# Outgoing sums in another pool's buffers, tied fetches, a gated conversion and one mask tile in a scan with two experts

## The chip, the cores and the metric

One core of one Trainium2 chip. The metric is the device time of one launch in microseconds, the median of three runs; a profiled execution of its own gives the trace.

## The reference

An attention with a running state, then two feed-forward experts one after the other on all 3072 tokens. Weights and inputs of the experts come as float64, the attention's as float32; all results are float32.

```
state = zeros(B, H, D, D)                       # B=4, H=8, D=40, S=768 steps
for t in range(S):
    y[:, :, t] = einsum('bhd,bhde->bhe', r[t], state)
    Sa = einsum('bhde,bhe->bhd', state, a[t])
    state = state * w[t][..., None, :] - einsum('bhd,bhe->bhde', Sa, b[t])
    state = state + einsum('bhd,bhe->bhde', v[t], k[t])
x = y as (3072, 320)
h = x @ w_in                                    # expert one, 320 x 2048
x = (max(h, 0) + alpha * min(h, 0)) @ w_out     # 2048 x 320
g = x @ w_gate                                  # expert two, 320 x 1536
out = (g * sigmoid(g) * (x @ w_val)) @ w_out2   # 1536 x 320
```

## The kernel before, in words

**Stages.** The 768 steps are cut into six blocks of 128 (`NM`), each in chunks of 64 (`L`), so that a block's scan is a row of matmuls with short steps of ScalarE and VectorE between them. Expert one of a block (512 tokens, `mlp1(j)`) can begin when the block's attention is there, and runs beside the scan of the following blocks to fill TensorE. Blocks 4 and 5 are left when the scan ends. Expert two runs over all six blocks at the end.

**Precision.** Each float32 factor is split into a high part and the rest (`split`: a copy on ScalarE, a subtraction on VectorE or GpSimd), and a product is a sum of three, so that one tile of 128 hidden units costs eight up matmuls (`up_mm`) and eight down matmuls (`down_mm`). An up product goes to the PSUM tile `u`, of which there is one in the scan and three afterwards; `prelu` makes `g` and its parts `gh`, `gl` from it; the down products are summed over the 16 tiles `f` of a block in `d0`, `d1`, `d2`.

**Weights.** A float64 weight is loaded as two words of 32 bits and made into a float32 by `narrow`: two operations on ScalarE, two on VectorE, in tiles `wy` (one buffer) and `wz` (two). `conv` then splits it. Expert one's converted weights go to a DRAM tile `wd` and are fetched as `wt` for each block (four buffers, `WB`); the tiles `f10` to `f15` are fetched in block 4 into tiles that stay for block 5 (`resident`, pool `hold`). Of expert two, four of twelve tiles are converted during the scan (`conv2`, 12 conversions, fetched back later) and 24 conversions (`direct`) follow after the scan straight into their resident tiles `w0`, `w1`, `w2`, some of them within expert two's first block.

**Sums of expert one.** At a block's end the three sums are copied from PSUM to a tile `x1o` and written to DRAM (`x1d`), two by ScalarE and the third, which adds two halves, by ScalarE and VectorE. `x1o` has the tag `xa`, the staging tile through which the next block's `x` is loaded (`fill_x`, three buffers). `g` has a pool `gp1` of two buffers, but is itself cut to one.

**Order.** The program is written as generators that `drive` interleaves by shares; a list scheduler then places each instruction by priority and by when its inputs and buffers come free, and every engine runs its own instructions in the order so found. All transfers named here are issued by SyncE, except the attention's stores `xd`, issued by ScalarE. A change of a pool's buffers moves instructions on all engines. `issue_after` is a tie in this scheduler: an instruction inside it is placed behind the named one where both are issued by one engine.

Of the kernel before, what the change touches and what calls it, by code (L numbers as in the profile page):

```python
# [39 lines left out]
ZB = 2  # L40
# [7 lines left out]
YB = 1  # L48
# [15 lines left out]
L = 64  # L64
HALF = 32
LOOK = 2
KEEP = 4

@with_exitstack
def kernel(  # L70
# [94 lines left out]
    def narrow(pool, raw):  # L165
# [8 lines left out]
        nc.vector.scalar_tensor_tensor(z, z, 3, y, ALU.logical_shift_left, ALU.bitwise_or)  # L174
        return f

    def split(raw, h, l, eng):
        nc.scalar.copy(out=h, in_=raw)  # L178
        eng.tensor_tensor(out=l, in0=raw, in1=h.bitcast(F32), op=ALU.subtract)  # L179

    def conv(stage, idx, src, f, kind, into=None):
        sw = words(src)
        if kind == "up":
            raw = stage.tile([128, 3, 128, 2], U32, tag="raw", name="raw", bufs=RB)
            sw = sw[:, f * 128:f * 128 + 128]
            nc.sync.dma_start(out=raw[:, 0:2], in_=sw[0:256].rearrange("(j p) n two -> p j n two", p=128))
            for p in (lo, hi):
                nc.sync.dma_start(out=raw[p, 2], in_=sw[256:DM])
        else:
            raw = stage.tile([128, DM, 2], U32, tag="raw", name="raw", bufs=RB)  # L190
            nc.sync.dma_start(out=raw, in_=sw[f * 128:f * 128 + 128])
        w32 = narrow(stage, raw)
        t = stage.tile([128, 768], F32R, tag="wc", name="wc", bufs=WCB) if into is None else into
        if kind == "up":
            t3 = t.rearrange("p (a b) -> p a b", a=6)
            split(w32, t3[:, 0:3], t3[:, 3:6], nc.gpsimd)
        elif kind == "down":
            split(w32[:, 0:256], t[:, 0:256], t[:, 256:512], nc.gpsimd)
            split(w32[:, 256:DM], t[:, 512:512 + RT], t[:, 512 + RT:2 * DM], nc.gpsimd)
        else:  # L200
            split(w32, t[:, 0:DM], t[:, DM:2 * DM], nc.gpsimd)
        if into is None:
            n = 768 if kind == "up" else 2 * DM
            nc.sync.dma_start(out=wd[idx, :, 0:n], in_=t[:, 0:n].bitcast(F32))

    fetched = []
    e1p = {}
    XAB = [XAB1]

    resident = {}  # L210

    def fetch(pool, idx, up, j):
        if idx in resident and j == NM - 1:
            return resident[idx]
        n = 768 if up else 2 * DM
        if j == NM - 1 or j == NM - 2 and idx >= 2 * HOLD:
            tag = f"w{idx // 2 % 2}" if up else "w2"
            t = e1p["hold"].tile([128, n], F32R, tag=tag, name="wt")
            resident[idx] = t.rearrange("p (a b) -> p a b", a=6) if up else t
        else:  # L220
            t = pool.tile([128, 768], F32R, tag="w", name="wt")
        fetched.append(nc.sync.dma_start(out=t[:, 0:n].bitcast(F32), in_=wd[idx, :, 0:n]))
        return t.rearrange("p (a b) -> p a b", a=6) if up else t

    def up_mm(ps, t, xs):
        xh, xl, xst = xs
        ops = []
        for j in range(2):
            ops += [(t[:, j], xh[:, j]), (t[:, j], xl[:, j]), (t[:, 3 + j], xh[:, j])]
        ops += [(t[:, 2], xst), (t[:, 5], xst)]  # L230
        for i, (lt, rh) in enumerate(ops):
            nc.tensor.matmul(ps, lt, rh, start=(i == 0), stop=(i == len(ops) - 1))  # L232

    def down_mm(ps, q, t, gh, gl, first, last):
        if q < 2:
# [31 lines left out]
        return xs  # L267

    def prelu(gpool, ps, f, n):
        g = gpool.tile([128, n], F32, tag="g", name="g", bufs=1)  # L270
        nc.scalar.activation(out=g, in_=ps, func=ACTF.Relu, scale=-1.0)  # L271
        nc.vector.scalar_tensor_tensor(g, g, neg[:, f:f + 1], ps, ALU.mult, ALU.add)  # L272
        gh = gpool.tile([128, n], F32R, tag="gh", name="gh")
        gl = gpool.tile([128, n], F32R, tag="gl", name="gl")
        split(g, gh, gl, nc.gpsimd if f % 16 < PGL else nc.vector)
        return gh, gl
# [18 lines left out]
    def mlp1(j, early=0):  # L295
# [5 lines left out]
        plan += [(f, 0, BLK) for f in fs if f >= early]  # L301
        dps = [psd.tile([128, BLK], F32, tag=f"d{q}", name=f"d{q}") for q in range(3)]
        pend = []

        def down(f, c0, c1, gh, gl):
            t = fetch(wp1, 2 * f + 1, False, j)
            for q in range(3):
                down_mm(dps[q][:, c0:c1], q, t, gh, gl, f == fs[0] and c0 == 0, f == fs[-1])

        seen = set()  # L310
        for f, c0, c1 in plan:
            if not seen & {(c0, c1), (0, half) if early and c0 == 0 else (c0, c1)}:
                with lifted():
                    b0, b1 = c0 // TB, c1 // TB
                    fill_x(xp1, xs, xd[j][:, b0:b1].rearrange("f b t -> f (b t)"), c0, c1)
                seen.add((c0, c1))
                yield
            t = fetch(wp1, 2 * f, True, j)
            ps = e1p["psu"].tile([128, c1 - c0], F32, tag="u", name="u")
            up_mm(ps, t, tuple(x[..., c0:c1] for x in xs))  # L320
            yield
            if len(pend) == DEP:
                down(*pend.pop(0))
            pend.append((f, c0, c1, *prelu(gp1, ps, f, c1 - c0)))
            yield
        for e in pend:
            down(*e)
        for q in range(3):
            tc.cur_priority -= XPRI
            o = xp1.tile([128, BLK], F32, tag="xa", name="x1o", bufs=XAB[0])  # L330
            if q < 2:
                nc.scalar.copy(out=o, in_=dps[q])
                nc.sync.dma_start(out=x1d[j][q * 128:q * 128 + 128], in_=o)
            else:
                nc.scalar.copy(out=o[lo], in_=dps[2][hi])
                nc.vector.tensor_tensor(out=o[lo], in0=dps[2][lo], in1=o[lo], op=ALU.add)
# [20 lines left out]
    WN = NSEG * (L + 1)  # L357
    wseg = rawp.tile([128, WN + 1], F32, name="wseg")
    nc.vector.memset(wseg[:, 0:WN + 1:L + 1], 0.0)
    reset = rawp.tile([128, NSEG // 2, L + 1], F32, name="reset")  # L360
    nc.gpsimd.memset(reset, 0.0)
    nc.gpsimd.memset(reset[:, :, 0:1], 1.0)
    first = rawp.tile([128, NSEG, L + 1], F32, name="first")
    nc.gpsimd.memset(first, 0.0)
    rests = [rawp.tile([128, NSEG, L + 1], F32, name=f"rest{j}") for j in range(2)]
    mask = pers.tile([128, L], F32, name="mask")

# [124 lines left out]
    def prep_a(i):  # L492
# [8 lines left out]
        for g in range(2):  # L501
# [395 lines left out]
    def direct():  # L897
        for f in range(KEEP, K2):
            for j, (held, src, kind) in enumerate(KINDS):
                t = wpool.tile([128, 768 if kind == "up" else 2 * DM], F32R, tag=f"w{j}", name=f"w{j}")  # L900
                conv(tail, 2 * K1 + 3 * f + j, src, f, kind, t)
                held[f] = t.rearrange("p (a b) -> p a b", a=6) if kind == "up" else t
                yield

# [123 lines left out]
```

## Time and profile before

| | us |
|---|---|
| median of 3 runs | 1274.12 (1267.84 to 1275.93) |
| profiled execution | 1273.08 |
| its span | 1271.0 |
| TensorE busy in it | 1110.3 |
| mean granted clock of TensorE | 0.929 of full |

The span is the time from the first to the last instruction that the profile shows; the profiled execution's own time has about 2 us outside it. In the rows PE is TensorE, DVE VectorE, ACT ScalarE, POOL GpSimd and SP SyncE. A row of a timeline is a run of equal instructions, and its bracket says how long the engine had been idle before and what released it.

### The profile page before, as it was taken

The page shows a single profiled execution, that of the slowest core. Times are in us where ns is not written, and L with a number is a line of the kernel's source. Part 1 is how long each engine was busy: PE and PEld are TensorE (multiplying, and loading weights), DVE is VectorE, ACT ScalarE, POOL GpSimd, SP SyncE. Part 2 cuts the span into 40 slices and gives each one's busy share as a digit, 9 for nine tenths or more (in the row PEclk, how much of TensorE's full clock was granted, in tenths as well). Part 3 has the DMA queues.
Part 4 walks back from the last instruction along what each step waited for, and adds up shares of the span by engine and source line. Part 5 has one row for each costly group of instructions (what it writes and reads, how often), then busy time and mean ns, then how long its engine had stood idle before and what let it go on. Part 6 is the DMA issues. An engine that isn't in the chain of part 4 may idle for free. (4 is left out here: it accounts for less than half of the span.)

```text
span 1271.0 us, 24355 instructions
## 1 busy us (share of the span) xinstructions
PE 1110.3 (87%) x9056; PEld 940.2 (74%) x9056; DVE 728.2 (57%) x1552; ACT 619.3 (49%) x1531; POOL 236.1 (19%) x405
## 2 busy tenths in 40 slices
PE   4146687999999989999899678998999999999998
PEld 4045676887777877787688555877888888888887
DVE  7798887688498579759554344457532323232222
ACT  4659468647745754863844334447432323232222
POOL 8336433311221221331321000003100000000000
PEclk9668677999999998999899889999999999999999
DMA  4535778555444554635765698245210101000000
GB/s 142 169 94 171 255 258 264 166 179 165 135 146 147 150 149 130 205 101 153 234 202 150 223 345 286 72 127 154 67 46 1 46 1 38 1 21 1 13 9 21
DMA packets 94885, 166.36 MB, mean 131 GB/s; under 512 B 13232, under 2 KB 43184, under 8 KB 94768
## 3 DMA queue, kind: packets, MB, share of 16 engines
q1 hardware_dynamic: 86608, 160.88, 40.1%
q10 hardware_dynamic: 8160, 3.93, 1.1%
q8 instruction: 72, 1.18, 0.4%
q14 instruction: 45, 0.37, 0.1%
HBM read 136.98 MB, written 27.79 MB: 130 GB/s over the span
## 5 line engine op out<-in xcount | busy, mean ns | idle before, releaser
L178 ACT CAST gh<-g 128x512 fp32r<-128x512 f32 (+1 forms) x176 | 105.6, 600 | 179.7 <-DVE g L964 120.5
L232 PE MATMUL u<-xh,wt 128*128 128x512 f32 (+1 forms) x416 | 153.1, 412 | 26.4 <-ACT xh L178 15.0
L179 DVE TENSOR_TENSOR gl<-g,gh 128x512 fp32r<-128x512 f32 (+1 forms) x176 | 118.6, 674 | 96.2 <-ACT gh L178 94.5
L964 DVE TENSOR_TENSOR g<-pv,sg 128x512 f32<-128x512 f32 x72 | 49.8, 692 | 215.6 <-PE pv L232 213.4
L272 DVE SCALAR_TENSOR_TENSOR g<-g,neg,u 128x512 f32<-128x512 f32 (+1 forms) x104 | 73.1, 703 | 96.4 <-ACT g L271 96.2
L232 PEld LDWEIGHTS u<-xh,wt 128*128 128x128 f32 x416 | 82.5, 202 | 50.2 <-ACT xh L178 15.7
L962 ACT ACTIVATE sg<-pg 128x512 f32<-128x512 f32 x72 | 43.0, 598 | 133.4 <-PE pg L232 133.4
L271 ACT ACTIVATE g<-u 128x512 f32<-128x512 f32 (+1 forms) x104 | 58.7, 565 | 98.3 <-PE u L232 70.5
L232 PE MATMUL pg<-xh,w 128*128 128x512 f32 x288 | 102.0, 394 | 3.6 <-ACT sg L962 3.6
L232 PE MATMUL pv<-xh,w 128*128 128x512 f32 x288 | 100.5, 389 | 0.0
L948 PE MATMUL o<-w,gh 128*128 128x320 f32 x288 | 87.3, 309 | 0.6 <-ACT gh L178 0.6
L949 PE MATMUL o<-w,gh 128*128 128x320 f32 x288 | 87.7, 309 | 0.0
L232 PE MATMUL u<-xl,wt 128*128 128x512 f32 (+1 forms) x208 | 82.8, 398 | 0.2 <-DVE xl L179 0.2
L238 PE MATMUL d<-gl,wt 128*128 128x512 f32 (+1 forms) x208 | 82.2, 397 | 0.0
L609 DVE TENSOR_TENSOR la<-la,tmp 128x96 f32<-128x96 f32 (+43 forms) x306 | 80.2, 290 | 2.0
L696 POOL COPY gs<-raw_v 64x160 f32<-64x160 f32 x96 | 45.1, 470 | 190.5 <-PE yp L753 94.9
L239 PE MATMUL d<-gh,wt 128*128 128x512 f32 (+1 forms) x208 | 80.2, 387 | 0.0
L601 DVE TENSOR_TENSOR tmp<-la 128x96 f32<-128x96 f32 (+43 forms) x306 | 78.9, 284 | 1.8
L540 PE MATMUL mnp<-AN,kbt 128*128 128x128 f32 x384 | 60.0, 309 | 22.6 <-DVE kbt L528 13.5
L950 PE MATMUL o<-w,gl 128*128 128x320 f32 x288 | 76.1, 309 | 0.0
L237 PE MATMUL d<-gh,wt 128*128 128x512 f32 (+1 forms) x208 | 70.9, 395 | 5.7 <-DMA wt<-wd 4.3
L554 POOL TENSOR_SCALAR_AFFINE_SELECT AN<-AN 64x256 f32<-64x256 f32 x96 | 51.5, 537 | 123.8 <-ACT AN L553 105.1
(116 smaller groups left out, 2575.8 us busy)
## 6 DMA issues: line engine op xcount, KB each, us to landing
wt<-wd SPq DMA_DIRECT2D x98, 384.0 KB
wt<-wd SPq DMA_DIRECT2D x98, 320.0 KB
wd<-wc SPq DMA_DIRECT2D x24, 384.0 KB
raw<-in_moe_w_out_dram SPq DMA_DIRECT2D x28, 320.0 KB
raw_bk<-in_bk_dram SPq DMA_DIRECT2D x48, 160.0 KB
wd<-wc SPq DMA_DIRECT2D x20, 320.0 KB
raw<-in_moe_w_in_dram SPq DMA_DIRECT2D x16, 256.0 KB
raw_v<-in_v_dram SPq DMA_DIRECT2D x24, 160.0 KB
```

Of the source, the lines that this page charges most:

```text
L178: nc.scalar.copy(out=h, in_=raw)
L179: eng.tensor_tensor(out=l, in0=raw, in1=h.bitcast(F32), op=ALU.subtract)
L232: nc.tensor.matmul(ps, lt, rh, start=(i == 0), stop=(i == len(ops) - 1))
L237: nc.tensor.matmul(ps, wh, gh, start=first, stop=False)
L238: nc.tensor.matmul(ps, wh, gl, start=False, stop=False)
L239: nc.tensor.matmul(ps, wl, gh, start=False, stop=last)
L272: nc.vector.scalar_tensor_tensor(g, g, neg[:, f:f + 1], ps, ALU.mult, ALU.add)
L601: nc.vector.tensor_tensor(out=tv, in0=ml[:, kk + 1:HALF, kk:kk + 1].to_broadcast([128, nr, ns]), in1=tl[:, kk:kk + 1, c0:c0 + ns].to_broad ...
L609: mark["inv"] = nc.vector.tensor_tensor(out=dst, in0=dst, in1=tv, op=ALU.subtract)
L948: nc.tensor.matmul(ops[q], gh[:, ts], wh, start=first, stop=False)
L949: nc.tensor.matmul(ops[q], gh[:, ts], wl, start=False, stop=False)
L950: nc.tensor.matmul(ops[q], gl[:, ts], wh, start=False, stop=last)
```

## The change

Four edits. The outgoing sums `x1o` take the tag `g` of pool `gp1` in place of `xa`, and `g` is no longer cut to one buffer, so that `g` and `x1o` share two. The fetches of the resident tiles stand in an `issue_after` on the up product three before (`AHEAD`). Expert two's 36 weights are converted by `gated`: three operations on VectorE put the word together, ScalarE takes an absolute value, and a comparison with a least value gives 0 or 1, by which the word is multiplied; the last two steps are two operations on GpSimd or, for every second one of the `direct` conversions (`dve`), one on VectorE. And `reset`, a mask for the scans with 1 at each chunk's start and 0 elsewhere, becomes a view of `first`, whose starts hold something else for a while in each use, so that 24 small memsets on VectorE put the 1 back.

```diff
+AHEAD = 3
...
+    LEAST = 1.125 * 2.0 ** -15
+    def gated(pool, raw, dve=0):
+        whi, wlo = raw[..., 1], raw[..., 0]
+        sh = list(whi.shape)
+        y = pool.tile(sh, U32, tag="wy", name="wy", bufs=YB)
+        z = pool.tile(sh, U32, tag="wz", name="wz", bufs=ZB)
+        f = z.bitcast(F32)
+        nc.vector.tensor_scalar(y, whi, 0x07FFFFFF, 3, ALU.bitwise_and, ALU.logical_shift_left)
+        nc.vector.scalar_tensor_tensor(z, whi, 0xC0000000, y, ALU.bitwise_and, ALU.bitwise_or)
+        nc.vector.scalar_tensor_tensor(y, wlo, 29, z, ALU.logical_shift_right, ALU.bitwise_or)
+        nc.scalar.activation(out=f, in_=whi.bitcast(F32), func=ACTF.Abs)
+        if dve:
+            nc.vector.scalar_tensor_tensor(f, f, LEAST, y.bitcast(F32), ALU.is_ge, ALU.mult)
+            return f
+        nc.gpsimd.tensor_scalar(f, f, LEAST, None, ALU.is_ge)
+        nc.gpsimd.tensor_tensor(out=f, in0=f, in1=y.bitcast(F32), op=ALU.mult)
+        return f
...
-        w32 = narrow(stage, raw)
+        w32 = narrow(stage, raw) if idx < 2 * K1 else gated(stage, raw, dve)
...
-        fetched.append(nc.sync.dma_start(out=t[:, 0:n].bitcast(F32), in_=wd[idx, :, 0:n]))
+        with tc.issue_after(done[-AHEAD].ins) if idx in resident and len(done) >= AHEAD else nullcontext():
+            fetched.append(nc.sync.dma_start(out=t[:, 0:n].bitcast(F32), in_=wd[idx, :, 0:n]))
...
-        g = gpool.tile([128, n], F32, tag="g", name="g", bufs=1)
+        g = gpool.tile([128, n], F32, tag="g", name="g")
...
-            o = xp1.tile([128, BLK], F32, tag="xa", name="x1o", bufs=XAB[0])
+            o = gp1.tile([128, BLK], F32, tag="g", name="x1o")
...
-    reset = rawp.tile([128, NSEG // 2, L + 1], F32, name="reset")
-    nc.gpsimd.memset(reset, 0.0)
-    nc.gpsimd.memset(reset[:, :, 0:1], 1.0)
     first = rawp.tile([128, NSEG, L + 1], F32, name="first")
     nc.gpsimd.memset(first, 0.0)
+    reset = first[:, 0:NSEG // 2]
+    nc.gpsimd.memset(reset[:, :, 0:1], 1.0)
...
+        nc.vector.memset(reset[:, :, 0:1], 1.0)
...
-                conv(tail, 2 * K1 + 3 * f + j, src, f, kind, t)
+                conv(tail, 2 * K1 + 3 * f + j, src, f, kind, t, (3 * f + j) % 2)
```

Counted in rows of the order, VectorE has 1552 instructions before and 1624 now, ScalarE 1456 and 1429, GpSimd 399 and 451. Three places of the new order follow; a number behind a name is the tile's own.

**SyncE at the scan's end.** `xa` with `xd4` or `xd5` are loads of `x` for blocks 4 and 5, `x1d3` the writes of block 3's sums. Before:

```order
L333 DMA x1d3_66<-x1o_8600 128x512 [waits DMAHW7_49,Activation_49]
L222 DMA wt_8815<-wd_69 128x768 [waits DMAHW0_49,PE_49]
L333 DMA x1d3_66<-x1o_8603 128x512 [waits DMAHW1_49,Activation_49]
L222 DMA wt_9584<-wd_69 128x640 [waits DMAHW2_49]
L222 DMA wt_9601<-wd_69 128x768 [waits DMAHW3_49]
L337 DMA x1d3_66<-x1o_8606 64x512 [waits DMAHW4_49,DVE_49]
L222 DMA wt_9612<-wd_69 128x640 [waits DMAHW5_49]
L222 DMA wt_9629<-wd_69 128x768 [waits DMAHW6_49]
L256 DMA xa_8680<-xd4_61 128x512 [waits DMAHW7_49]
```

Now, some 65 rows ahead of those writes, and then around them:

```order
L279 DMA xa_8716<-xd4_61 128x512 [waits DMAHW7_49,DMAHW3_49,DMAHW1_49]
L279 DMA xa_8720<-xd4_61 128x512 [waits DMAHW4_49]
L283 DMA xa_8724<-xd4_61 64x512 [waits DMAHW5_49]
L283 DMA xa_8724<-xd4_61 64x512 [waits DMAHW6_49]
L507 DMA raw_vt0_159<-in_vt_dram 40x512 [waits DMAHW0_49,Activation_49]
```

```order
L357 DMA x1d3_66<-x1o_8628 128x512 [waits Activation_49]
L244 DMA wt_8874<-wd_69 128x640 [waits DMAHW5_49,PE_49]
L357 DMA x1d3_66<-x1o_8631 128x512 [waits Activation_49]
L361 DMA x1d3_66<-x1o_8634 64x512 [waits DMAHW7_49,DVE_49]
L279 DMA xa_9785<-xd5_62 128x512 [waits DMAHW2_49,DMAHW5_49,DMAHW1_49,DMAHW6_49,DMAHW0_49,DVE_49]
L279 DMA xa_9789<-xd5_62 128x512 [waits DMAHW3_49]
L283 DMA xa_9793<-xd5_62 64x512 [waits DMAHW4_49]
L283 DMA xa_9793<-xd5_62 64x512
L244 DMA wt_8929<-wd_69 128x768 [waits PE_49]
L244 DMA wt_9591<-wd_69 128x768 [waits DMAHW7_49,DVE_49]
```

The loads of block 4's `x` have moved from behind the first write to far ahead of it; block 5's stand right behind the writes now. At the three boundaries before, the next block's loads have moved ahead of the writes likewise. From the first load of block 5's `x` to the weights of block 4's down product `f8`, SyncE issues 23.59 MB before (44 `wt`, 4 of `w0` and `w1`, 12 pieces of `x`, 20 of raw weights, 3 writes) and 19.07 MB now (40 `wt`, 13 pieces of `x`, 13 of raw weights). On TensorE 64 up products of expert one and 62 down products stand ahead of the scan's end before, 65 and 64 now; ahead of the end of the scan's last stage but one it is 55 and 54 before, 62 and 61 now.

**ScalarE at the same place.** `xh` are casts of `x`. Before:

```order
L178 CAST gh_8551<-g_8548 128x512 [waits DVE_49]
L178 CAST xh_9733<-xa_9739 128x512 [waits DMAHW1_49,DMAHW7_49,DMAHW0_49,Pool_49]
L332 COPY x1o_8600<-d0_7110 128x512 [waits PE_49]
L178 CAST xh_9733<-xa_9743 128x512 [waits DMAHW1_49]
L332 COPY x1o_8603<-d1_7111 128x512 [waits PE_49]
L335 COPY x1o_8606<-d2_7112 64x512 [waits PE_49]
L261 CAST xst_9735<-xa_9747 128x512 [waits DMAHW3_49,DMAHW2_49]
L178 CAST xh_8674<-xa_8680 128x512 [waits DMAHW7_49]
```

Now:

```order
L356 COPY x1o_8628<-d0_7135 128x512 [waits PE_49,Activation_49]
L356 COPY x1o_8631<-d1_7136 128x512 [waits DVE_49,PE_49]
L359 COPY x1o_8634<-d2_7137 64x512 [waits DMAHW2_49,PE_49,Activation_49]
L797 DMA xd5_62<-pv_9189 40x4x128 [waits DMAHW5_49,DVE_49]
L797 DMA xd5_62<-pv_9189 40x4x128 [waits DMAHW6_49]
L294 ACTIVATE g_8774<-u_8731 128x512 [waits DMAHW4_49,Activation_49]
L797 DMA xd5_62<-pv_9194 40x4x128 [waits DMAHW0_49,DVE_49]
L797 DMA xd5_62<-pv_9194 40x4x128 [waits DMAHW1_49]
L198 CAST gh_8777<-g_8774 128x512 [waits DVE_49]
L294 ACTIVATE g_8828<-u_8809 128x512 [waits DMAHW7_49,PE_49]
```

The third copy and the two Relus behind it wait for transfers (DMAHW) now, and two of them stand ahead of the attention's stores `xd5`.

**GpSimd and VectorE in the late conversions.** GpSimd before:

```order
L179 TENSOR_TENSOR w0_10382<-wz_10388,w0_10382 128x384 [waits DMAHW7_49,Activation_49]
L179 TENSOR_TENSOR w2_10371<-wz_10375,w2_10371 128x320 [waits DMAHW6_49,Activation_49]
L179 TENSOR_TENSOR w1_10395<-wz_10401,w1_10395 128x384 [waits Activation_49]
L179 TENSOR_TENSOR w2_10446<-wz_10450,w2_10446 128x320 [waits DMAHW2_49,PE_49,Activation_49]
L179 TENSOR_TENSOR w0_10457<-wz_10463,w0_10457 128x384 [waits DMAHW0_49,Activation_49]
```

GpSimd now:

```order
L199 TENSOR_TENSOR w0_10197<-wz_10203,w0_10197 128x384 [waits Activation_49]
L193 TENSOR_SCALAR wz_10310<-wz_10310 128x384 [waits Activation_49]
L194 TENSOR_TENSOR wz_10310<-wz_10310,wy_10309 128x384 [waits DVE_49,Pool_49]
L199 TENSOR_TENSOR w1_10304<-wz_10310,w1_10304 128x384 [waits Activation_49]
L193 TENSOR_SCALAR wz_10380<-wz_10380 128x384 [waits Activation_49]
L194 TENSOR_TENSOR wz_10380<-wz_10380,wy_10379 128x384 [waits DVE_49,Pool_49]
L199 TENSOR_TENSOR w0_10374<-wz_10380,w0_10374 128x384 [waits DMAHW0_49,PE_49,Activation_49]
```

VectorE now, in the same stretch (`g` and `gl` with `neg` are `prelu`'s):

```order
L199 TENSOR_TENSOR gl_9914<-g_9910,gh_9913 128x512 [waits PE_49,Activation_49]
L187 SCALAR_TENSOR_TENSOR wz_10395<-raw_10390,wy_10394 128x384 [waits Pool_49]
L188 SCALAR_TENSOR_TENSOR wy_10394<-raw_10390,wz_10395 128x384 [waits DVE_49]
L199 TENSOR_TENSOR gl_9938<-g_9934,gh_9937 128x512 [waits PE_49,Activation_49]
L295 SCALAR_TENSOR_TENSOR g_9972<-g_9972,neg_76,u_9941 128x512 [waits Activation_49]
L191 SCALAR_TENSOR_TENSOR wz_10395<-wz_10395,wy_10394 128x384 [waits Activation_49]
L186 TENSOR_SCALAR wy_10432<-raw_10430 128x320 [waits DMAHW1_49,DVE_49]
L295 SCALAR_TENSOR_TENSOR g_9998<-g_9998,neg_76,u_9981 128x512 [waits Activation_49]
L187 SCALAR_TENSOR_TENSOR wz_10433<-raw_10430,wy_10432 128x320 [waits DVE_49,Pool_49]
L199 TENSOR_TENSOR gl_9976<-g_9972,gh_9975 128x512 [waits PE_49,Activation_49]
L188 SCALAR_TENSOR_TENSOR wy_10432<-raw_10430,wz_10433 128x320 [waits DVE_49]
```

On GpSimd a conversion has one or three steps where it had one, and on VectorE steps that wait for GpSimd (Pool) or ScalarE stand ahead of `prelu`'s. Of the 24 late conversions 15 stand ahead of expert two and 9 within its first seven tiles.

## Rows read from the trace of the kernel before

**Rows 1.** The page's section 1: busy time of each engine.

```profile
PE 1110.3 (87%) x9056; PEld 940.2 (74%) x9056; DVE 728.2 (57%) x1552; ACT 619.3 (49%) x1531; POOL 236.1 (19%) x405
```

**Rows 2.** Windows: span, PE, PEld, DVE, ACT, POOL busy (instructions), clock, DMA share, GB/s.

```profile
330.00:360.00 30.00, 25.30 (x270) 20.52 (x269) 16.67 (x42) 22.36 (x69) 8.08 (x19) 0.95 0.46 138
460.00:492.00 32.00, 25.34 (x270) 20.32 (x269) 30.32 (x90) 14.13 (x40) 6.72 (x14) 0.84 0.53 159
600.00:630.00 30.00, 24.34 (x479) 19.64 (x478) 21.07 (x39) 23.88 (x57) 9.79 (x13) 0.88 0.69 212
...
745.00:785.00 40.00, 31.70 (x127) 22.57 (x126) 20.58 (x31) 18.32 (x36) 4.96 (x5) 1.00 1.02 366
785.00:880.00 95.00, 91.68 (x392) 72.85 (x390) 49.40 (x70) 46.56 (x86) 11.29 (x11) 1.00 0.35 108
...
910.00:1271.00 361.00, 355.42 (x1841) 312.50 (x1839) 98.56 (x144) 95.34 (x167) 0.00 (x0) 1.00 0.05 17
```

**Rows 3.** Timeline of PE, scan's end: start, duration, operation, [idle before, releaser].

```profile
712.97 0.61 PE L757 MATMUL yp<-rbd,s 128*64 128x128 f32 x8
...
734.78 2.08 PE L232 MATMUL u<-xh,wt 128*128 128x512 f32 x4 [14.83 <-ACT xh L178]
...
788.47 0.62 PE L237 MATMUL d<-gh,wt 128*128 128x512 f32 x2
...
880.89 0.50 PE L232 MATMUL pg<-xh,w 128*128 128x512 f32 x1 [3.61 <-ACT sg L962]
```

**Rows 4.** Timeline of PE inside the scan, waits behind block boundaries.

```profile
354.91 0.67 PE L705 MATMUL zp<-gs,AN 128*64 128x40 f32 x16 [1.79 <-DVE pv L765]
...
472.16 1.65 PE L715 MATMUL pp<-tt,zs 128*64 128x64 f32 x32 [1.50 <-ACT zs L707]
...
477.87 0.69 PE L723 MATMUL pp<-ident,ut 128*128 128x128 f32 x2 [3.01 <-ACT pv L719]
...
624.77 0.67 PE L705 MATMUL zp<-gs,AN 128*64 128x40 f32 x16 [1.71 <-DVE pv L765]
627.24 1.98 PE L715 MATMUL pp<-tt,zs 128*64 128x64 f32 x32 [1.81 <-ACT zs L707]
```

**Rows 5.** Timeline of SP: issues at block 0's end and the scan's.

```profile
338.00 0.33 SPq L333 DMA_DIRECT2D x1d<-x1o  x1
...
340.40 2.84 SPq L256 DMA_DIRECT2D xa<-xd  x2
...
716.96 0.80 SPq L256 DMA_DIRECT2D xa<-xd  x2
...
721.90 0.32 SPq L333 DMA_DIRECT2D x1d<-x1o  x1
...
728.04 0.32 SPq L256 DMA_DIRECT2D xa<-xd  x1
```

**Rows 6.** Timeline of ACT: block 4's cast of x, block 4's outgoing sums.

```profile
734.11 0.62 ACT L178 CAST xh<-xa 128x512 fp32r<-128x512 f32 x1 [10.09 <-DMA xa<-xd]
...
814.82 1.07 ACT L332 COPY x1o<-d 128x512 f32<-128x512 f32 x2 [1.26 <-PE d L239]
```

**Rows 7.** Groups by line: busy us, mean ns; the last from 850-908.

```profile
L178 ACT CAST gh<-g 128x512 fp32r<-128x512 f32 (+1 forms) x176 | 105.6, 600 | 179.7 <-DVE g L964 120.5 <-DVE g L272 45.8 <-PE d L239 6.8
...
L174 DVE SCALAR_TENSOR_TENSOR wz<-wz,wy 128x384 uint32<-128x384 uint32 (+1 forms) x68 | 36.3, 534 | 2.3
...
L359 DVE MEMSET wseg<- 128x9 f32 x1 | 0.1, 66 | 0.9 <-PEq L1015 0.9
...
L179 POOL TENSOR_TENSOR w<-wz,w 128x384 fp32r<-128x384 f32 (+1 forms) x17 | 17.2, 1015 | 62.3 <-ACT w L178 62.3
```

**Rows 8.** Timeline of DVE, then of POOL, conversions in block 4.

```profile
746.34 0.56 DVE L173 SCALAR_TENSOR_TENSOR wy<-raw,wy 128x384 uint32<-128x384 uint32 x1
...
748.52 1.08 DVE L173 SCALAR_TENSOR_TENSOR wy<-raw,wy 128x384 uint32<-128x384 uint32 x1 [0.43 <-ACT wy L172]
...
748.17 1.02 POOL L179 TENSOR_TENSOR w<-wz,w 128x384 fp32r<-128x384 f32 x1 [55.91 <-DMA wt<-wd]
```

More of the change, by code (lines that the diff above doesn't have):

```diff
@@ L179, in split, with conv @@
         eng.tensor_tensor(out=l, in0=raw, in1=h.bitcast(F32), op=ALU.subtract)
-    def conv(stage, idx, src, f, kind, into=None):
+    def conv(stage, idx, src, f, kind, into=None, dve=0):
         sw = words(src)
@@ L206 @@
     fetched = []
+    ups = []
     e1p = {}
@@ L210, with fetch @@
     resident = {}
-    def fetch(pool, idx, up, j):
+    def fetch(pool, idx, up, j, done=()):
         if idx in resident and j == NM - 1:
@@ L231, in up_mm @@
         for i, (lt, rh) in enumerate(ops):
-            nc.tensor.matmul(ps, lt, rh, start=(i == 0), stop=(i == len(ops) - 1))
+            last = nc.tensor.matmul(ps, lt, rh, start=(i == 0), stop=(i == len(ops) - 1))
+        return last
     def down_mm(ps, q, t, gh, gl, first, last):
@@ L303, in mlp1 @@
         pend = []
+        done = ups
         def down(f, c0, c1, gh, gl):
-            t = fetch(wp1, 2 * f + 1, False, j)
+            t = fetch(wp1, 2 * f + 1, False, j, done)
             for q in range(3):
@@ L317, in mlp1 @@
                 yield
-            t = fetch(wp1, 2 * f, True, j)
+            t = fetch(wp1, 2 * f, True, j, done)
             ps = e1p["psu"].tile([128, c1 - c0], F32, tag="u", name="u")
-            up_mm(ps, t, tuple(x[..., c0:c1] for x in xs))
+            done.append(up_mm(ps, t, tuple(x[..., c0:c1] for x in xs)))
             yield
```

## The prediction

> **What bounds the kernel now.** I read the busy line of the page first: TensorE works 1110.3 of the 1271.0 us span, VectorE 728.2, ScalarE 619.3, GpSimd 236.1 [rows 1]. TensorE is the bound, so the question is where its missing 161 us lie and which of them the change can reach. The table of windows answers that by stage [rows 2]. From 910 us on (expert two) TensorE is busy 355.42 of 361 us at a granted clock of 1.00: nothing to gain there, and the change doesn't touch its products. 785 to 880 (block 5 of expert one) has 91.68 of 95. What is left are two kinds of places. First, the stretches behind a block boundary inside the scan: 330 to 360, 460 to 492 and 600 to 630 have 25.30, 25.34 and 24.34 us busy, at clocks of 0.95, 0.84 and 0.88. Second, the stage after the scan's end: 745 to 785 has 31.70 of 40 us busy with the DMA share at 1.02 and 366 GB/s, so TensorE waits for weights there.
>
> Ahead of that lies one hole. The scan's last products start at 712.97 and run 0.61 us (end 713.58); the first up product of block 4 starts at 734.78, after 14.83 us in which TensorE waited for a cast of `x` [rows 3]. Followed back: that cast ran at 734.11 after ScalarE had waited 10.09 us for the load [rows 6]; the load was issued only at 728.04, since its staging tile `xa` had held a sum on its way out, whose write was issued at 721.90 [rows 5]: 6.1 us for the write to land in a queue full of fetches. The same tile is shared at every boundary; in the quieter queue at block 0's end it cost 340.40 - 338.00 = 2.4 us [rows 5].
>
> **The change part by part.** The sum is made against the profiled execution: 1273.08 us, of which 1271.0 are span (2.08 outside); the median, 1274.12, is 1.04 above it.
>
> *Sums leave from `g`'s buffers.* In the new order, the loads of the next block's `x` stand some 65 rows ahead of the three `x1d` writes on SyncE; before they stood behind them. Two effects, priced apart.
>
> (a) Boundaries inside the scan. The waits of the scan's own chain that TensorE couldn't fill there are 1.79, 1.50, 3.01, 1.71 and 1.81 us, 9.8 in all [rows 4]: with `x` at hand an up product (8 matmuls; 91.68 us / 392 = 0.234 each, so 1.87 us [rows 2]) fits into such a hole. The clock below full is worth at most 30 x 0.05 + 32 x 0.16 + 30 x 0.12 = 10.2 us [rows 2]. The ceiling is 20 us; I take two thirds, 13, since some of the chain's waits end before a product would. Against it stands a new wait: `x1o` takes three turns in two buffers, so ScalarE's third copy waits until the first write has landed, and the next Relu until the second has, with the scan's own ScalarE work queued behind. At the quiet 2.4 us less two copies (1.07 us for two [rows 6]) this is 1.3 each, 4 for three boundaries. Net -9; bounds -20 and +3 (the 6.1 us write at all three: 3 x 5 = 15 against 13, rounded up).
>
> (b) Scan end to the down product of `f8` in block 4, the point at which the backlog of loads is used up. Before: 788.47 - 713.58 = 74.9 us [rows 3]. From the first load of block 5's `x` (716.96 [rows 5]) the queue carries 23.59 MB until that product's weights (44 `wt`, 4 `w0`/`w1`, `x` pieces, raw weights, the three writes), 64.5 us at 366 GB/s; the product starts 788.47 - 716.96 = 71.5 after it, so 7.0 are start-up and its up product. In the new order it is 40 `wt`, no `w0`/`w1`, 13 raw pieces instead of 20, no write: 19.07 MB, 52.1 us. TensorE has `x` of block 4 at the scan's end and works through this stretch while weights come; its own work there is 2 x 9 products x 1.87 = 34 us, under 52, so the queue sets the pace. The first load moves from 3.4 to about 5.4 us after the scan's end, because on ScalarE the scan's last stores now stand behind the third `x1o` copy and its wait (2.4 us again, part of it beside the last products). New: 5.4 + 52.1 + 7.0 = 64.5, a gain of 10.4. But the new order puts one up and two down products more before the scan's end, 3 x 1.87 = 5.6, so that end is later. Net -4.8, rounded -5; bounds -11 (the queue at 400 GB/s, my guess for a best case) and 0 (the stretch is as long as before but for those products).
>
> (c) Block 5's end. Before, two copies took 1.07 us from 814.82 on [rows 6] and the rest followed without a wait. Now the third copy waits until the first copy's write has been issued and has landed, 0.33 + 2.4 us after that copy, and the next Relu for the second's landing, half a copy's pair later; VectorE's step and a cast follow before the next down product. That is about 4 us later than before less what up products in flight cover, 1. Price +3, bounds 0 and +6.
>
> *Fetches tied behind up products.* The tie orders a fetch behind a matmul, but the fetch is issued by SyncE and the matmul by TensorE; the order of all five engines is the same with the tie as without it, and no wait on TensorE stands on the fetches of the resident tiles because of it. Price 0.
>
> *Gating.* For 36 conversions ScalarE loses one operation, which I count at nothing, since it is the bound in none of these stages; VectorE gains 48 operations (one in each, one more in the 12 that finish there); GpSimd gains 48 (two in each of 24). VectorE's cost 0.56 us alone and 1.08 where GpSimd works at the same time [rows 8]: 27 to 52 us. GpSimd's two have no row of their own; bounds 0.51 (half of its two-input step, for the one with one input) and 1.015 us [rows 7]: 24 to 49 us. Both engines have room over the whole span; what hides it is TensorE's own work in blocks 4 and 5, VectorE being busy 49.40 of 95 us there [rows 2]. `wy` has one buffer and is now held until the last multiply, so a conversion holds it some 3 x 0.56 + 0.53 + 2 x 1.01 = 4.2 us against about 3.4 before (17 in 58 us [rows 7]). 15 of the 24 late conversions come before expert two, 9 within its first seven tiles: 9 x 4.2 = 38 us against 7 x 5.4 of product time there (72 tiles in 1271 - 881 us [rows 3]), so they just keep up. I take +3 for late ones and VectorE held ahead of `g`; bounds -1 and +8.
>
> The first row says the cover can be lost: VectorE's step takes 1.08 instead of 0.56 when GpSimd's is running [rows 8]. The Trainium skill ("GPSIMD Engine Reference", Engine selection) speaks against putting elementwise work on GpSimd: about twice as slow as VectorE for two inputs; the rows agree, 1.015 against 0.534 us. By that page the multiply alone would be better left on VectorE.
>
> *One mask tile.* 24 small memsets more on VectorE. The nearest rows are a 128x9 memset at 0.066 us and, as an upper end, the two-input step of 0.534 [rows 7]: 1.6 to 13 us; nearest to the memset. In 460 to 492 VectorE is busy 30.32 of 32 us [rows 2], so there it lies on the path, as do the third operations of the 12 conversions that run inside the scan. +2, bounds 0 and +6.
>
> Sum: -9 - 5 + 3 + 0 + 3 + 2 = -6. Span 1265, plus 2.08 is 1267, plus 1.04 for the median: **1268 us**.
>
> **The rivals.**
>
> *Seamless* (chance 0.27). The early `x` fills every hole and keeps the clock up: (a) -16, (b) -9, the rest 0 to +3. For it: by the second last stage of the scan the new order has seven `f` more of expert one done. Against it: these products also push the scan back. -25 to -13; as one number -19, 1255 us.
>
> *Slower through VectorE behind GpSimd* (0.13). In the new order VectorE's second step of a conversion waits for GpSimd, with `g` of the next prelu queued behind it. A tile's up and down products give 3.7 us of cover; the prelu chain itself takes four steps of about 0.65 (its cast 0.600 [rows 7], VectorE's somewhat longer). It decides once the wait exceeds the remaining 1.1 us; two GpSimd steps of 1.01 then cost 0.9 to 2.0 in each of some 10 conversions in blocks 4 and 5, and the pairing of rows 8 lengthens them. Price 16 in place of 3: +7, 1281 us, and up to 1290. The Trainium skill ("Advanced Engine Details and Errata", GPSIMD Details) says that GpSimd shares a read and a write interface with VectorE and collides with its steps of two SBUF inputs. 0.56 against 1.08 us is that case.
>
> *Writes in the way* (0.12). A landing takes the 6.1 us of row 721.90 rather than 2.4 at every boundary, since fetches fill the queue. ScalarE stands still 4.9 us at each, with the scan behind it: (a) +2, (c) +6, sum +8: 1282 us. It decides when more than some 0.9 MB is queued ahead of the write (2.4 us at 366 GB/s).
>
> *The change doesn't do what it says*: for the tie that is part of the forecast already, at no cost.
>
> **How the numbers follow.** Forecast 0.48 (1261 to 1276), seamless 0.27, VectorE 0.13, writes 0.12. One per cent, what a measurement of this kernel can tell, is 1261.4 and 1286.9. Faster: seamless and the forecast's lower end, 0.30; slower: a third of the two slow cases and something unseen (any change here reshuffles the whole order), 0.13; same 0.57. The range cuts the ends of seamless and of the slow cases: 1252 to 1285.
>
> **What would show it.** Right: no 14.83 us hole after the scan, block 4's first up product within 2 us of its end; the waits of rows 4 shorter; ScalarE idle 1 to 3 us before the third `x1o` at each boundary, ended by a DMA; the down product of `f8` some 65 us after the scan's end with the queue near 366 GB/s; conversions 4 to 5 us apart; the resident fetches where they were relative to the queue. Wrong: TensorE waiting for VectorE's `g` in block 5, idle over 4 us at each boundary, or expert two waiting for converted weights after 910.

## The result, and the profile after

1260.53 us median (1257.29 to 1263.61, six runs) against 1272.05 of before in the same comparison: ratio 0.9911, 95% interval 0.9885 to 0.9938. The kernel became faster by 11.5 us, twice what was forecast and inside the range. The profiled execution of the changed kernel took 1257.29 us, with a span of 1255.3; it is its fastest run, 3 us under the median. So the two profiled executions lie 15.8 us apart and not 11.5.

First the windows over the changed kernel, with those of [rows 2] and one for the whole scan; columns as there:

```profile
200.00:700.00 500.00, 470.01 (x5140) 394.12 (x5138) 369.91 (x904) 304.84 (x835) 138.27 (x250) 0.98 0.56 172
330.00:360.00 30.00, 29.25 (x274) 24.44 (x272) 20.39 (x59) 17.61 (x52) 8.22 (x20) 1.00 0.49 139
460.00:492.00 32.00, 27.22 (x269) 21.17 (x268) 31.05 (x99) 17.63 (x51) 3.71 (x7) 1.00 0.53 156
600.00:630.00 30.00, 27.44 (x455) 22.36 (x453) 18.10 (x34) 20.52 (x45) 15.97 (x19) 1.00 0.71 231
745.00:785.00 40.00, 32.67 (x127) 25.01 (x127) 20.80 (x33) 13.48 (x24) 7.88 (x8) 0.91 0.67 233
785.00:880.00 95.00, 82.19 (x354) 66.66 (x353) 54.37 (x85) 41.42 (x75) 24.73 (x23) 0.95 0.36 110
910.00:1255.00 345.00, 339.56 (x1760) 298.63 (x1758) 94.79 (x138) 91.63 (x161) 0.00 (x0) 1.00 0.06 18
```

And the windows over the kernel before, for the whole scan:

```profile
200.00:700.00 500.00, 465.52 (x5030) 388.47 (x5030) 352.58 (x868) 301.33 (x826) 114.44 (x225) 0.95 0.54 165
```

Across the scan TensorE is busy 470.01 us in place of 465.52, at a clock of 0.98 in place of 0.95: 4.5 us less idle, and 0.03 x 467 = 14 us of work more from the clock. The three stretches behind boundaries are at 1.00 now. They alone have 8.9 us less idle time (8.1 in place of 17.0) and 10.2 of the 14 us of clock; in the rest of the scan TensorE idles 4.4 us more. The boundaries themselves lie earlier now, so here are 30 us each from the first copy of an outgoing sum (blocks 0, 1 and 2) on, before:

```profile
337.40:367.40 30.00, 25.26 (x237) 20.82 (x237) 23.14 (x61) 20.22 (x59) 5.98 (x14) 0.94 0.50 152
467.60:497.60 30.00, 23.34 (x240) 18.50 (x239) 27.99 (x87) 16.26 (x47) 4.03 (x9) 0.83 0.52 154
604.40:634.40 30.00, 24.34 (x437) 19.86 (x436) 18.35 (x30) 24.68 (x60) 10.63 (x14) 0.83 0.74 234
```

And now:

```profile
324.50:354.50 30.00, 30.00 (x292) 25.40 (x292) 18.26 (x50) 20.06 (x58) 9.30 (x22) 1.00 0.49 142
460.30:490.30 30.00, 25.22 (x259) 19.72 (x259) 29.63 (x94) 16.77 (x48) 3.71 (x7) 1.00 0.53 155
586.60:616.60 30.00, 26.32 (x493) 21.16 (x491) 20.42 (x53) 19.84 (x45) 9.62 (x14) 0.94 0.41 119
```

TensorE idles 17.1 us in them before and 8.5 now. Behind the scan the picture turns: 785 to 880 has 82.19 us busy where it had 91.68 of 95.

The timeline of PE from the scan's end on answers to [rows 3]:

```profile
699.49 0.61 PE L781 MATMUL yp<-rbd,s 128*64 128x128 f32 x8
702.56 0.50 PE L254 MATMUL u<-xh,wt 128*128 128x512 f32 x1 [2.46 <-DVE g L295]
...
730.15 0.77 PE L254 MATMUL u<-xh,wt 128*128 128x512 f32 x1 [5.54 <-DMA wt<-wd]
...
760.85 0.76 PE L260 MATMUL d<-gh,wt 128*128 128x512 f32 x1 [1.20 <-ACT g L294]
...
793.35 0.80 PE L254 MATMUL u<-xh,wt 128*128 128x512 f32 x1 [4.14 <-DVE g L295]
...
846.59 0.50 PE L254 MATMUL pg<-xh,w 128*128 128x512 f32 x1
...
864.70 0.79 PE L254 MATMUL pg<-xh,w 128*128 128x512 f32 x1 [8.67 <-ACT sg L986]
```

The scan ends at 700.10 (713.58 before). The hole of 14.83 us is gone; in its place stand 2.46 us for `g`, 5.54 us for weights and smaller waits. 760.85 is the down product of `f8`: 60.8 us after the scan's end, 74.9 before. Then two new waits: 4.14 us at block 4's end, and 8.67 us at the start of expert two, where 3.61 stood; they are all that TensorE idles between 785 and 880.

What those last ones wait for, in the timeline of ACT:

```profile
696.15 1.07 ACT L356 COPY x1o<-d 128x512 f32<-128x512 f32 x2 [1.11 <-PE d L262]
698.87 0.58 ACT L359 COPY x1o<-d 64x512 f32<-64x512 f32 x1 [1.65 <-DMA x1d<-x1o]
...
701.13 0.60 ACT L294 ACTIVATE g<-u 128x512 f32<-128x512 f32 x1 [1.67 <-DMA x1d<-x1o]
...
788.55 1.07 ACT L356 COPY x1o<-d 128x512 f32<-128x512 f32 x2 [4.93 <-PE d L262]
791.30 0.58 ACT L359 COPY x1o<-d 64x512 f32<-64x512 f32 x1 [1.67 <-DMA x1d<-x1o]
...
853.83 1.07 ACT L356 COPY x1o<-d 128x512 f32<-128x512 f32 x2
...
857.51 0.58 ACT L359 COPY x1o<-d 64x512 f32<-64x512 f32 x1
...
862.75 1.28 ACT L986 ACT_TABLE_LOAD   x1 [0.56 <-DMA x1d<-x1o]
864.05 1.09 ACT L986 ACTIVATE sg<-pg 128x512 f32<-128x512 f32 x2
```

At the ends of blocks 3 and 4 the third copy of a sum stands 1.7 us for the first one's write (L359 behind `x1d<-x1o`), as the new order had it; at block 0's end it is 1.33 us, and at those of blocks 1 and 2 other work of ScalarE stands between the copies. At the last boundary the copies are also queued between conversions, the third write can only be issued at 860.18, and the first Silu's table load, queued behind them all, starts when that write has landed, after 0.56 us of idling. With the span cut at the scan's end and at expert two's first product (846.59; 867.82 before), to the last matmul's end, the profiled runs give:

| us | to the scan's end | to expert two | to the last matmul |
|---|---|---|---|
| before | 713.6 | 154.2 | 397.6 |
| after | 700.1 | 146.5 | 403.0 |
| difference | -13.5 | -7.8 | +5.4 |

### The profile page after: what moved, and what is told of

Read it like the earlier page. It is cut to its first block, busy times and chain, and to the rows that moved or that the text cites. A ratio compares the mean times of both kernels' runs of the same rounds, so it can differ in the third digit from the quotient of the medians.

```text
span 1255.3 us, 24461 instructions
## 1 busy us (share of the span) xinstructions
PE 1100.4 (88%) x9056; PEld 936.4 (75%) x9056; DVE 754.6 (60%) x1624; ACT 605.0 (48%) x1495; POOL 282.0 (22%) x452
## 4 chain that ended last, share of the span: by engine, by line
PE 57%; DMA 9%; DVE 8%; ACT 7%; issue 2%; POOL 1%; SPq 1%; ACTq 0%; DVEq 0%; POOLq 0%
PE pg L254 10%; PE pv L254 10%; PE u L254 9%; PE o L973 3%; PE o L972 3%; PE o L974 3%; PE d L260 2%; DMA wt<-wd 2%; PE d L261 2%; PE d L262 2%; PE gp L762 2%; DMA raw<-in_moe_w_gate_dram 2%; PE yp L777 1%; PE mnp L564 1%; DMA xd<-pv 1%
## 5 line engine op out<-in xcount | busy, mean ns | idle before, releaser
L199 DVE TENSOR_TENSOR gl<-g,gh 128x512 fp32r<-128x512 f32 (+1 forms) x176 | 122.0, 693 | 93.7 <-ACT gh L198 88.9
L262 PE MATMUL d<-gh,wt 128*128 128x512 f32 (+1 forms) x208 | 81.0, 391 | 0.0
L720 POOL COPY gs<-raw_v 64x160 f32<-64x160 f32 x96 | 42.2, 439 | 172.5 <-PE yp L777 110.8
L260 PE MATMUL d<-gh,wt 128*128 128x512 f32 (+1 forms) x208 | 73.7, 407 | 5.3 <-DMA wt<-wd 4.1
```

Source lines behind the costliest of these rows:

```text
L260: nc.tensor.matmul(ps, wh, gh, start=first, stop=False)
L262: nc.tensor.matmul(ps, wl, gh, start=False, stop=last)
```

## The experiments

The theory at first was the prediction's: the sums' place makes the gain. The rivals: `g`'s second buffer, gating, or the mere order.

**1. Order at the start** (`reset` made after `first` in the kernel before, nothing else):

```diff
-    reset = rawp.tile(...); nc.gpsimd.memset(reset, 0.0); nc.gpsimd.memset(reset[:, :, 0:1], 1.0)
     first = rawp.tile(...); nc.gpsimd.memset(first, 0.0)
+    reset = rawp.tile(...); nc.gpsimd.memset(reset, 0.0); nc.gpsimd.memset(reset[:, :, 0:1], 1.0)
```

> The kernel before with nothing changed but the place of two memsets at the program's start (the tile first is made before reset, not after), which lets the scheduler order thousands of rows differently. Theory (the move of the outgoing sums shortened the scan and the stage after it): 1272 us within 4, hole of 13 to 16 us after the scan as before. Rival (any new order moves this kernel by such amounts, the parts of the change mean little): off by more than 6 us, either way.

1287.49 us, ratio 1.0116 (1.0091 to 1.0141): 15 us slower, with a hole of 21.15 us. The rival holds: the order alone moves the kernel by more than the change did.

**2. Sums back in `xa`**, `g` with two buffers:

```diff
-            o = gp1.tile([128, BLK], F32, tag="g", name="x1o")
+            o = xp1.tile([128, BLK], F32, tag="xa", name="x1o", bufs=XAB[0])
```

> The changed kernel with the outgoing sums back in the staging tile xa; g keeps its second buffer, gating and the one mask stay. Theory (the sums' place makes the gain): 1268 to 1276 us, a hole of more than 8 us between the scan's end and block 4's first up product, scan end near 712, and no wait of TensorE for g at block 5's end. Rival (the second buffer of g makes the gain): 1257 to 1264 us, scan end near 700.

1265.42 us, 0.9939 (0.9914 to 0.9963). Under the theory's band, with its hole back (15.01 us) and the scan's end at 712.5.

**3. And `g` back to one buffer** (`tag="g", name="g", bufs=1`):

> As the run before, and g back to one buffer: only gating, mask and tie are left of the change. Theory (sums' place): 1270 to 1278 us, as before plus a few us for the late conversions. Rival (gating, which takes one operation per conversion from ScalarE, makes the gain): 1257 to 1264 us. Rival (second buffer of g): slower than the run before by 8 us or more.

1243.80 us, 0.9777 (0.9750 to 0.9805): faster than before and after, without the moved sums. The scan ends at 701.55, and block 4's first product waits 3.62 us. The timeline of its PE there:

```profile
700.94 0.61 PE L781 MATMUL yp<-rbd,s 128*64 128x128 f32 x8
705.17 0.60 PE L254 MATMUL u<-xh,wt 128*128 128x512 f32 x1 [3.62 <-ACT xh L198]
```

SP of the same kernel:

```profile
697.74 0.86 SPq L357 DMA_DIRECT2D x1d<-x1o  x2
699.55 0.47 SPq L361 DMA_DIRECT2D x1d<-x1o  x1
701.56 0.99 SPq L279 DMA_DIRECT2D xa<-xd  x2
```

In this order block 3's sums are written at 697.74 to 699.55, ahead of the scan's end, and nothing is queued in front of the loads of `x` behind them. So the hole can vanish, and the time fall further, without the moved sums; my theory, that their place makes the gain, doesn't hold as it stood. What is left of it is weighed below.

**4. No gating** (`narrow` for all weights in the changed kernel):

> The changed kernel with the old conversion for expert two's weights; the sums' place, the second buffer, the mask and the tie stay. Theory (gating only costs, at the late conversions): 1254 to 1260 us, expert two's first wait of 8.67 us down to under 5. Rival (gating gives a part of the gain): 1264 us or more.

1260.50 us, 0.9904 (0.9881 to 0.9928), as with gating; first wait of expert two 10.86 us, not under 5. Neither expectation held.

**5 and 6. The mask alone, and gating alone, on the kernel before:**

> The kernel before with the one mask tile alone (the 24 small memsets added). Theory A (the mask edit itself brings the scan forward: the four runs that had it wrote block 0's first sum at 324 to 325 us, the two without it at 337 and 343): 1240 to 1256 us, block 0's first sum near 325. Theory B (the order that the scheduler happens to find sets the time, no part by itself): anywhere from 1245 to 1290; block 0's first sum not tied to 325.

> The kernel before with the gated conversion alone. Theory A: 1268 to 1278 us, block 0's first sum at 337 or later, since the mask edit is missing. Theory B: anywhere from 1245 to 1290. Rival C (gating is what made the third run fast): 1240 to 1252 us.

1268.03 us, 0.9979 (0.9962 to 0.9995), and 1263.45 us, 0.9942 (0.9921 to 0.9962). The mask brings block 0's first sum to 329 (337 before), yet the scan ends at 718.8, the latest of all. Each alone gives little, both together gave 28 us in run 3: the parts don't add up, which speaks for theory B.

**7. Sums of blocks 4 and 5 in the staging tiles that exist after the scan**, the changed kernel otherwise, its order the same almost to the scan's end:

```diff
-            o = gp1.tile([128, BLK], F32, tag="g", name="x1o")
+            o = gp1.tile([128, BLK], F32, tag="g", name="x1o") if j < NM - 2 else e1p["xp"].tile([128, BLK], F32, tag="xa", name="x1o", bufs=4)
```

> The changed kernel, but the sums of blocks 4 and 5 go out from the staging tiles that exist after the scan (four buffers), so that the order is the same almost to the scan's end. Theory (at blocks 4's and 5's ends the sums in g's buffers cost waits for writes, 4.14 us of TensorE at 793 and about 5 of the 8.67 at 864, and a colder clock behind them): 1248 to 1253 us, both waits under 2 and 4 us. Rival (what waits there is hidden by what comes later, the queue or the conversions): 1258 to 1262 us.

1243.36 us, 0.9789 (0.9764 to 0.9813): 17.2 us under the changed kernel by the medians, 15.5 by the two ratios, 10.3 between the profiled executions. The timeline of its PE:

```profile
785.84 1.65 PE L254 MATMUL u<-xh,wt 128*128 128x512 f32 x3 [4.08 <-ACT xh L198]
...
856.02 0.50 PE L254 MATMUL pg<-xh,w 128*128 128x512 f32 x1 [0.18 <-ACT sg L986]
```

ACT of the same kernel:

```profile
853.48 0.58 ACT L359 COPY x1o<-d 64x512 f32<-64x512 f32 x1
854.08 1.28 ACT L986 ACT_TABLE_LOAD   x1
855.38 0.60 ACT L986 ACTIVATE sg<-pg 128x512 f32<-128x512 f32 x1
```

The third copy, table load and Silu follow each other without a wait, and expert two loses 0.18 us where it lost 8.67; from its first product to the end it takes 392.8 us (403.0). The wait at block 4's end stayed at 4.08: block 5's `x` now stands behind the sums there. So the theory is right for block 5's end; at block 4's end another wait took the place of the first, and what the sums cost there this run doesn't tell.

**8. Run 3 with one memset done twice** (`nc.gpsimd.memset(first, 0.0)` repeated):

> The kernel of the third run (sums in the staging tile, one g; gating and mask kept) with one memset on GpSimd at the start done twice, 0.5 us of work, which changes the order of most rows. Theory B (order alone): 1250 us or more, as a single draw of a wide spread does not come out at 1244 twice. Theory A (the edits it keeps make it fast): 1241 to 1248 us.

1273.38 us, 1.0013 (1.0000 to 1.0027): all of run 3's gain is gone, and a hole of 16.87 us is back, ended by a weight's fetch this time.

**9. A tie that acts**, on the kernel before: the resident fetches behind the last load of block 4's `x`, both issued by SyncE:

```diff
-        fetched.append(nc.sync.dma_start(...))
+        with tc.issue_after(mark[NM - 2].ins) if idx in resident else ExitStack(): fetched.append(nc.sync.dma_start(...))
```

> The kernel before with a tie that does act: the fetches of the resident tiles are ordered on SyncE behind the last load of block 4's x, so that the x1d3 writes and these loads go through an empty queue; the order ahead of the scan's end is the one of before. Theory (after the scan the queue of weights sets the pace, so the hole of 14.83 us was mostly cover for it): the hole shrinks to 7 to 9 us, the weights of block 5 come as much later, time 1270 to 1278. Rival (the hole is TensorE time lost): 1263 to 1267 us.

1271.55 us, 1.0002 (0.9985 to 1.0018). The timeline of its PE:

```profile
730.86 0.79 PE L232 MATMUL u<-xh,wt 128*128 128x512 f32 x1 [11.07 <-ACT xh L178]
...
736.70 0.76 PE L232 MATMUL u<-xh,wt 128*128 128x512 f32 x1 [2.45 <-DMA wt<-wd]
...
768.70 0.47 PE L232 MATMUL u<-xh,wt 128*128 128x512 f32 x1 [4.50 <-DMA wt<-wd]
```

The hole is 11.07 us, not 7 to 9: the first product of block 4 came 4 us earlier, and the time with weights missing later gave it back (4.50 us at 768.70): expert two starts at 867.95 us, 867.82 before. So the 3.8 us of hole were cover for the queue, as the theory has it; what the rest of it costs this run doesn't tell.

**10 and 11. The kernel of run 7, and the changed kernel, each with that memset done twice:**

> The kernel of the run with the late sums elsewhere, with one memset at the start done twice, as in the run of the third kernel. Theory (order of the scan is a draw, worth up to 15 us either way; the waits at blocks 4's and 5's ends are worth some 17 us in any order): anywhere from 1235 to 1270, and 10 to 20 us below the next run, which differs from this one only in those sums. Rival (the 17 us were a draw too): no fixed distance to the next run.

> The changed kernel with the same memset done twice. Theory: within 15 us of 1260 either way, and 10 to 20 us above the run before. Rival (the changed kernel's 1260 is what its edits are worth, whatever the order): 1258 to 1263 us.

1258.80 us, 0.9887 (0.9870 to 0.9905), and 1270.40 us, 0.9978 (0.9957 to 0.9998). Distance 11.6 us; expert two takes 392.8 and 403.5 us, the same 10 as between run 7 and after. So that cost is the same in another order. The changed kernel with one memset more is nearly as slow as before, but the memset isn't neutral. The timeline of DVE in the changed kernel:

```profile
8.21 1.35 DVE L525 TENSOR_TENSOR_SCAN rest<-wseg,first 128x260 f32<-128x260 f32 x2 [3.66 <-ACT wseg L520]
```

The same instruction in run 11:

```profile
11.14 1.36 DVE L525 TENSOR_TENSOR_SCAN rest<-wseg,first 128x260 f32<-128x260 f32 x2 [6.59 <-POOL first L387]
```

The first scan starts 2.9 us later, since the small memset on `first` is put behind others on GpSimd; by the first `dps` product (85.61 and 91.95) it is 6.3 us. In run 10 against run 7 it is 6.8 us by then, in run 8 against run 3 it is 3.4. The doubled memset cost 9.9, 15.4 and 29.6 us in runs 11, 10 and 8 by the medians, 8.5, 12.5 and 30.0 by the ratios. If that early delay lasts to the end, some 3, 7 and 26 us are left for the order, and the first of them isn't clear of the noise. Run 1 has no such delay by then (87.08 against 86.62), so its 15 us are the order's.

**12. Run 7 with the 24 late conversions by `narrow`**, those in the scan gated:

```diff
-        w32 = narrow(stage, raw) if idx < 2 * K1 else gated(stage, raw, dve)
+        w32 = narrow(stage, raw) if idx < 2 * K1 or into is not None else gated(stage, raw, dve)
```

> The run with the late sums elsewhere, and the 24 conversions after the scan done the old way; the 12 in the scan stay gated, so that the order ahead of the scan's end is the same. Theory (late gating is hidden up to a few us): 1238 to 1244 us against 1243.4. Rival (gating helps late, by taking work from ScalarE): 1246 us or more.

1251.60 us, 0.9824 (0.9801 to 0.9848): 8.2 us slower than run 7 by the medians, the rival's side; by the ratios it is 4.5 us, with intervals that overlap a little. The windows of run 7:

```profile
840.00:880.00 40.00, 39.81 (x195) 33.88 (x194) 29.89 (x47) 19.80 (x38) 18.77 (x16) 1.00 0.47 139
```

Those of run 12:

```profile
840.00:880.00 40.00, 36.35 (x170) 30.05 (x169) 29.21 (x41) 27.47 (x56) 12.35 (x12) 1.00 0.52 158
```

And its PE:

```profile
864.10 0.50 PE L254 MATMUL pg<-xh,w 128*128 128x512 f32 x1 [2.88 <-ACT sg L986]
```

ScalarE works 27.47 of 40 us instead of 19.80, the copies of block 5's sums wait among the conversions' steps (859.58, 851.09 in run 7), and TensorE waits 2.88 us for the first Silu.

## Why the prediction was right or wrong

Direction and range held; the sum of -6 was too small and its parts were off in both directions. In the forecast's terms the profiled executions give -19 for (a), -8.5 for (b) and +11.8 from `f8` on, where +6 stood for (c) and gating: -15.7 in all, against 11.5 by the medians.

**(a) Boundaries in the scan, -9: right in place and mechanism, too small in this profile.** The scan ended 13.5 us earlier with 5.6 us of products more ahead of it, so 19 in all, at the bound of -20. The three stretches that I had named hold as much (8.9 us of idle time and 10.2 of clock), and I had taken two thirds of that ceiling, less 4 for new waits. The size hangs on the execution, though. In runs 7 and 12, whose order is the same up to there, the scan ended at 707.9 and 709.9 us, which makes 11 and 9 us by the same count. Whether it is owed to the early `x` can be asked of all fourteen profiles, sorted by where the sums of blocks 0 to 3 go. The clock below full is 30 us times what the granted clock lacks to 1.00, summed over the three boundaries:

| us | sums in `g` (after, runs 4, 7, 10, 11, 12) | sums in `xa` (before, runs 1, 2, 3, 5, 6, 8, 9) |
|---|---|---|
| TensorE idle in the 3 x 30 us | 7.2 to 11.4 | 12.8 to 17.3 |
| clock below full there | 1.7 to 7.4 | 4.3 to 11.9 |
| hole ahead of block 4's first product | 0.8 to 2.8 | 3.6 to 21.2 |
| scan's end | 700.1 to 717.8 | 701.6 to 718.8 |
| expert one's matmuls ahead of it | 1160 in each | 1065 to 1152 |

The idle time at the boundaries separates the groups, as the forecast has it. The scan's end doesn't, but in the right column up to 95 matmuls less stand ahead of it, 22 us at the forecast's 0.234 each. This fits term (a) and doesn't prove it: every edit changes the order too, and the columns hold only three and seven different orders. The new waits on ScalarE at these boundaries are there, 1.33 us at 327 for instance, but small as said.

**(b) Scan end to `f8`, -5: right in mechanism.** 60.8 us against 64.5 forecast. The queue is full in this stretch in both kernels (DMA share 0.97 and 0.96), before and then now:

```profile
713.60:788.50 74.90, 49.92 (x193) 36.34 (x194) 31.04 (x47) 27.81 (x52) 4.96 (x5) 0.89 0.97 338
700.10:760.85 60.75, 42.83 (x161) 32.36 (x161) 25.77 (x43) 19.57 (x34) 8.02 (x8) 0.90 0.96 337
```

The rate is 338 and 337 GB/s over the whole stretch, where I had reckoned with 366.

**(c) +3: the wait was right, its second place was left out.** The term is headed as block 5's end, but its row, 814.82 us, is block 4's, and there 4.14 us came. At block 5's end no price was set, and there the same wait, with the conversions queued between the copies, made 8.67 us of 3.61. This is the step that failed. Removing the late part gave 17.2 and 11.6 us by the medians (runs 7 and 10 against after and 11), 10.1 and 10.7 of which lie behind expert two's first product. That last stretch is the one in which two edits show in every order. From expert two's first product to the last matmul the profiles take, in us:

| | last sums in `g` | last sums elsewhere |
|---|---|---|
| gated | 403.0, 403.5 (after, run 11) | 392.8 to 394.9 (runs 2, 3, 6, 7, 8, 10) |
| `narrow` | 405.3 (run 4) | 397.1 to 400.1 (before, runs 1, 5, 9, 12) |

**Tie, 0: not contradicted, and not tested.** It was not run by itself; run 9's tie, which acts, is worth nothing either.

**Gating, +3: wrong in sign.** From expert two's first product on it gains some 4 us with the last sums elsewhere and 2 with them in `g`, whatever the order, by the table. In the whole time it is 8.2 or 4.5 us in run 12 (the 2.88 us and the 0.76 ahead of expert two, 0.18 in run 7, are a part of it; the rest stays open), and 0.0 with the sums in `g` and another order (run 4). That ScalarE's relief counts for nothing was the error: it is ScalarE that carries the copies and the Silu at the last boundary. The slower rival, VectorE behind GpSimd, shows in one place, 2.18 us at 757.15, and no more. GpSimd's steps did cost more than the upper bound (51.3 us against 49), by the groups of the changed kernel (busy us, mean ns):

```profile
L193 POOL TENSOR_SCALAR wz<-wz 128x384 f32<-128x384 f32 (+1 forms) x24 | 27.5, 1145 | 92.9 <-ACT wz L189 86.1 <-DVE g L295 5.6 <-DVE x1o L360 1.0
...
L194 POOL TENSOR_TENSOR wz<-wz,wy 128x384 f32<-128x384 f32 (+1 forms) x24 | 23.8, 993 | 1.8
...
L186 DVE TENSOR_SCALAR wy<-raw 128x384 uint32<-128x384 uint32 (+1 forms) x36 | 12.7, 352 | 24.7 <-POOL wz L194 17.0 <-DMA raw<-in_moe_w_gate_dram 3.5 <-DMA wt<-wd 3.1
...
L187 DVE SCALAR_TENSOR_TENSOR wz<-raw,wy 128x384 uint32<-128x384 uint32 (+1 forms) x36 | 26.9, 746 | 3.8 <-POOL w L199 2.4
...
L535 DVE MEMSET first<- 128x4 f32 x24 | 1.5, 62 | 1.0
```

1.145 us for the one-input step (bounds 0.51 and 1.015). A memset is 0.062 us, 1.5 in all, at the lower end.

So the 11.5 us are what was saved at the boundaries and up to `f8`, less late waits that cost some 10, give or take what the order happens to be: two memsets in another place moved the kernel before by 15 us. That the early `x` made the saving fits all fourteen profiles and isn't proved. That the misses of (a) and (c) partly cancel is luck. Which of the scheduler's choices makes one order's scan end at 702 and another's at 718 stays open; some 10 us of such a spread come with the order unchanged (700.1, 707.9 and 709.9). The hole is 14 to 21 us in before and runs 1, 2, 6 and 8, 11 in run 9, 8 in run 5 and under 4 in the others, but most of it is made good later. From the scan's end to expert two TensorE idles 23.0 to 29.0 us in the six kernels with 11 us of hole or more, and 17.0 to 22.4 in the seven with less than 4; before and after it is 25.6 and 22.1. Run 7's version, at 1243.36, beats both kernels, as does run 3's; by runs 8 and 10 some of that is order as well. Among the rivals, the listed parts of *Seamless* come to -25 to -22 us, while its range reaches to -13.

## What to carry to other kernels

Where a scheduler writes the order, measure first what a nearly neutral reordering does: here 15 and some 26 us in two cases, both times slower, so an edit worth less can't be judged by the total of one build. Compare the same stage over all builds instead: idle time behind a boundary and the length of the last stage told the edits apart where the totals didn't. Buffers that free a load make someone else wait for a write: look at the last boundary, where nothing is left to cover it. And a hole in front of a stretch that a queue bounds is for the most part not time to be had.

## What the runs showed of the hardware

GpSimd's one-input step was slower than its two-input step (1.145 against 0.993 us). VectorE's one-input step took 0.352 us on average. Its two-input step L187 (mean 0.746) on 128x384 took 0.53 to 0.56 us in 18 of 24 cases and 1.04 to 1.25 in six, and what decides is which engine started first. The six started 0.22 to 0.41 us behind a two-input step of GpSimd that still ran; in eight cases GpSimd's step came up to 0.20 us behind VectorE's, and VectorE's kept its time. One pair, VectorE and then GpSimd:

```profile
642.58 0.56 DVE L187 SCALAR_TENSOR_TENSOR wz<-raw,wy 128x384 uint32<-128x384 uint32 x1
643.17 1.12 DVE L188 SCALAR_TENSOR_TENSOR wy<-raw,wz 128x384 uint32<-128x384 uint32 x1
642.59 1.28 POOL L199 TENSOR_TENSOR wc<-wz,wc 128x320 fp32r<-128x320 f32 x1 [1.06 <-ACT wc L198]
```

The Trainium skill ("Advanced Engine Details and Errata", GPSIMD Details) names steps with two SBUF inputs as those that collide, which these rows bear out. Three kernels with the same order up to their scan's end (after, runs 7 and 12) reached it at 700.1, 707.9 and 709.9 us, with clocks of 0.98, 0.96 and 0.96 between 200 and 700: the granted clock differs from run to run by that much.
